# A transformer chain on one core: weight chunks held behind the latest gelu, late chunks packed into four periods, low weight parts from DRAM

## The chip, the core and the metric

The kernel runs on one core of one Trainium2 chip. The metric is the device time of one launch in microseconds; smaller is better. The program has five engines that run their own instruction queues in order: TensorE (PE, matmuls and transposes), VectorE (DVE), ScalarE (ACT), GpSimd (POOL) and SyncE (SP, which here issues nearly all DMA transfers). They wait for each other by semaphores.

## The reference

```python
attn = softmax(rotate(q) @ rotate(k).T / sqrt(64)) @ v          # 4 batches, 8 heads, 576 tokens
h = gelu(x @ w_in); u, v = h[..., :512], h[..., 512:]            # x: [4, 576, 512]
v_s = w_sg @ (layernorm(v) * g_ln) + b_sg
x = x + (u * v_s) @ w_out                                        # the gated block
u = x + (x.T @ U @ V).T
out = u + relu(u @ w_ch1) @ w_ch2                                # the channel block, 512 -> 2048 -> 512
```

All inputs are float32; weights reach the kernel as 64-bit words.

## The kernel before

**Stages.** Attention fills the first 320 us, the gated block (one batch after the other) runs to about 545 us, the channel block to the end. Every float32 operand is split into a high part (rounded) and a low part (the rest), and a product is three matmuls: high by high, low by high, high by low. High parts are copies on ACT, low parts subtractions on DVE or POOL.

**Weight chunks.** `w_ch1` and `w_ch2` come as 64-bit words, and DVE turns them into float32. One chunk is a DMA load of raw words, an `Abs` on ACT (`begin`, line 774 of before), and four DVE instructions (`rest`, lines 770 to 773). After two chunks (four of the late ones, which are half as large) `combine` makes four sums (lines 781 to 784), and the seven operands of one Strassen-like scheme go to DRAM (`COMBO`, tile `cb`, `cb3`). 26 chunks are converted during the gated block by `first_weights`; there a scheduler chooses each engine's order by its own time model, and `issue_after(x)` makes it put an instruction behind `x` on the same engine. The other 12 half chunks are converted during the channel block at the times of the table `LATE`.

**The gated block's v step.** `v_step` multiplies, ACT applies gelu out of PSUM (`ug<-v`, line 578, which frees the PSUM tile), DVE takes mean and variance (`bst`, `bmv`), POOL the reciprocal root (`brs`), ACT normalises (line 640) and copies the high part (`VH`). `u_step` has its gelu at line 659. `o_step` accumulates `w`, `y_step` transposes it (`t`, copies `YH` on ACT) and `z_step` multiplies the transposes.

**The channel block.** It has 12 periods of 14 steps, one product of 12 matmuls each; period i handles token block p and hidden group g of `ORDER[i]`. Steps 0 to 6 make `u @ w_ch1` (operands `UOP` times `W1`, into PSUM tiles rx, ry, rz), steps 7 to 13 the second product (`ROP` times `W2`, into aX, ry, rz). Between them DVE and ACT build `ROP` in a strict chain: at step time 1.0 ACT copies rx ("p1", PE's step 2 may write rx only then), at 2.0 DVE adds it to ry (tile `t`), at 2.5 ACT applies relu, at 3.0 ACT copies rx again ("u2", PE's step 4 waits), at 4.0 ACT copies rz ("p5", step 5 waits), at 5.0 DVE adds rx to it (step 6 waits). In this block all engines but PE follow an order written out by hand: each action has a time in steps, `at(t, fn)`, and the list sorted by time is each engine's program order; an engine reaches an action when its queue does, not at that time.

**Weights of the next period.** `split` loads operands from `COMBO` into a staging tile (`YH`, `YL`: four tiles in rotation), ACT copies the high part and the low part is made from the same staging tile. For a hidden group that was used before ("not fresh": the changes into the groups of periods 4, 5, 7 and 8), low parts listed in `KEPT` come from DRAM (`LOWS`) instead, written there in periods 0 to 2. Before the change these were two of the seven low parts of `W1` and all of `W2`; POOL made the other five of `W1` after r7l in the second half of periods 3, 4, 6 and 7. `UKEPT` keeps the token operands (`u` in the DMA rows) the same way at the times of `KEEP`.

Of the kernel before, what the change touches and what calls it, by code (L numbers as in the profile page):

```python
# [12 lines left out]
AF = mybir.ActivationFunctionType  # L13
# [52 lines left out]
def tile_kernel(ctx: ExitStack, tc: tile.TileContext, qk, vv, tabs, w_in, g_ln, wsgT, b_sg, w_out, u_r, v_r, w1, w2, out):  # L66
    nc = tc.nc

    def f(ap):
        return ap.bitcast(F32)  # L70

    def h2(ap):
        return ap.rearrange("p (a b) -> p a b", a=2)
# [26 lines left out]
    HALF = S // 2  # L100
# [315 lines left out]
    for h in range(2, NH):  # L416
        t = NC * h
# [123 lines left out]

    LASTS, LAST_G, LAST_D = [None] * 3, [None], [None]
    TAILS = []
# [32 lines left out]
    def gelu(t, ps):  # L576

        nc.scalar.activation(t, ps, AF.Gelu_apprx_tanh)
        return t
# [72 lines left out]
    def u_step(b, k0):  # L652
        ps = ps_tile(f"u{b}_{k0}")
        pr = []
        for k in range(KT):
            wh, wl = WUH[:, k, k0 * P:(k0 + 1) * P], WUL[:, k, k0 * P:(k0 + 1) * P]
            pr += [(wh, XH[:, k]), (wh, XL[:, k]), (wl, XH[:, k])]
        mm3(ps, pr, 2)
        nc.scalar.activation(h2(ug[:, k0]), ps[:, :, :HALF], AF.Gelu_apprx_tanh)

# [90 lines left out]
    ORDER = [(0, 0), (0, 1), (0, 2), (1, 2), (1, 0), (1, 1), (2, 1), (2, 0), (2, 2), (2, 3), (0, 3), (1, 3)]  # L751
    KEPT = [(0, 0), (0, 1)] + [(1, j) for j in range(7)]
    LOWS = [[dram.tile([P, 7, FG], F32, name=f"lows{c}_{g}", bufs=1) for g in range(NG - 1)] for c in range(2)]
# [81 lines left out]
    def first_u():  # L835
# [15 lines left out]
    LATE = (  # L851
        (36.0, 42.1, "t"), (50.0, 56.1, "t"), (55.7, 57.8, "s"), (48.0, 59.2, "w"), (64.0, 70.1, "t"), (78.0, 84.1, "t"), (74.0, 85.8, "w"),
        (92.0, 98.1, "t"), (90.0, 101.7, "w"), (106.0, 112.1, "t"), (111.7, 113.6, "s"), (104.5, 115.0, "w"),
    )
    FIRST = {9: (-11, 1.3, 1.8), 10: (-10.9, 1.7, 2.1), 11: (-10.8, 2.2, 2.6), 12: (-10.7, 2.7, 3.1), 13: (3.2, 5.2, 5.6)}
    KEEP = {
        0: ((1, 8.0), (2, 9.0)), 1: ((6, 8.0), (5, 9.0)), 2: ((7, 0.1), (3, 1.0), (4, 2.0)), 4: ((1, 8.0), (2, 9.0)),
        5: ((6, 0.1), (5, 0.6), (7, 1.1), (3, 1.6), (4, 2.1)),
    }

    def channel(before):
# [15 lines left out]
        def wslot(c, x, j, n=1):  # L877
            if c == 0 and j >= 5:
                return seta[2 * (j - 5) + x]
            return (W1, W2)[c][x][:, j:j + n].rearrange("p a b -> p (a b)")  # L880
# [16 lines left out]
        def at(t, fn):  # L897
            events.append((t, len(events), fn))
# [48 lines left out]
        def period(i):  # L947
# [71 lines left out]
            if g not in [x for _, x in ORDER[:i]] and g < NG - 1:  # L1019
                for c, j in KEPT:  # L1020
                    at(o + (0.05 if c == 0 else 8.0 if i in (0, 2) else 3.5), lambda c=c, j=j: nc.sync.dma_start(LOWS[c][g][:, j], f(wslot(c, 1, j))))
            if h != g:
                fresh = h not in [x for _, x in ORDER[:i]]
                loads = (2.3, 4.0, 4.5, 6.5, 6.6) if i == 0 else (0.2, 0.3, 1.3, 2.4, 5.0) if i > 3 else (1.4, 1.8, 3.2, 3.5, 5.0)
                highs = (3.85, 5.45, 6.5, 9.0, 9.4) if i == 0 else (3.85, 4.75, 6.0, 7.0, 9.4)
                for c, j0, j1, load, t, lo, e in (
                    (0, 0, 2, loads[0], highs[0], 4.35, dve), (0, 2, 4, loads[1], highs[1], 10.3, pool),
                    (0, 4, 6, loads[2], highs[2], 11.6, pool), (0, 6, 7, loads[3], highs[3], 12.9, pool),
                    (1, 0, 2, loads[4] + (i == 8), highs[4], 14.5, dve), (1, 2, 4, 11.65, 13.0, 15.08, dve),
                    (1, 4, 6, 13.0, 15.1, 16.5, dve), (1, 6, 7, 13.6, 16.2, 17.1, dve),  # L1030
                ):
                    if fresh or (c, j0) not in KEPT:
                        split(c, h, j0, j1, o + t, stage, o + load, o + lo, e)
                    else:
                        split(c, h, j0, j1, o + t, stage, o + load, o + 7 * c + j1 + 0.05)
# [12 lines left out]
            def combo(n, a, b):  # L1048
# [5 lines left out]
                      "l4": 17.35, "h1": 1.7, "h2": 2.1, "h6": 6.3, "h5": 6.7, "h3": 9.9, "h7": 15.9, "h4": 16.8} if i < 4 else  # L1054
                     {"T5": 1.0, "T6": 1.5, "T7": 1.95, "T4": 2.4, "l1": 2.9, "l2": 3.35, "l6": 3.8, "l5": 4.6, "l7": 14.1, "l3": 14.55,
                      "l4": 15.0, "h1": 1.7, "h2": 2.1, "h6": 3.1, "h5": 4.1, "h3": 6.3, "h7": 7.2, "h4": 9.9})
            parts = {5: (b12, b11), 6: (b22, lambda: U[5]), 7: (b12, b22), 4: (b21, lambda: U[6])}
# [33 lines left out]
        def leave_combo(m):  # L1091
            c, r, _, _ = parts[m]
            nc.sync.dma_start(COMBO[c][NG - 1][:, :, r], cbs[m // 4])
        for m, (load, t, _) in enumerate(LATE):
            at(load, lambda m=m: fetch(m))
            at(t - 0.1, lambda m=m: begin(m))
            at(t, lambda m=m: raws[m][1]())
            if m % 4 == 3:
                at(t + 0.75, lambda m=m: combine(parts[m][0], cbs[m // 4]))
                at(t + 1.5, lambda m=m: leave_combo(m))  # L1100
        for i in range(len(ORDER)):
# [182 lines left out]
```

## Time and profile before

| quantity | value |
| --- | --- |
| median of 3 runs | 936.46 us (935.14 to 937.0) |
| the profiled execution, its own time | 932.18 us |
| its span (first to last instruction) | 930.4 us |
| PE busy in the span | 892.5 us (96%) |
| DVE, ACT, POOL busy | 749.5, 463.6, 427.3 us |
| granted TensorE clock, mean | 0.991 |

Times in the rows below count from the start of the span. A row "[1.99 <-ACT ug L578]" says that the engine stood idle 1.99 us before it, and which instruction released it.

### The profile page before, as it was taken

To read this page: it belongs to the slowest core of one execution; us is meant where nothing else is said; L and a number is where in the kernel's file an instruction comes from. 1 tells how busy PE (TensorE), PEld (TensorE's weight loads), DVE (VectorE), ACT (ScalarE), POOL (GpSimd) and SP (SyncE) were. 2 spreads that over 40 slices of the span, in tenths; PEclk is the share of its full clock that TensorE was granted. 3 is DMA by queue.
4 is the path that set the end of the run, shared out by engine and by line. 5 is a ranking of instruction groups with operands and counts; after the bars stand their busy time and mean duration, and the time that the engine had idled before them with its cause. 6 is when DMAs were issued, how large, how long until landed. Compare 5 with 4: busy or idle time off the path is not lost. (4 is left out here: it accounts for less than half of the span.)

```text
span 930.4 us, 14303 instructions
## 1 busy us (share of the span) xinstructions
PE 892.5 (96%) x5279; PEld 804.7 (86%) x5279; DVE 749.5 (81%) x991; ACT 463.6 (50%) x719; POOL 427.3 (46%) x322
## 2 busy tenths in 40 slices
PE   8999999999999998899999988999999998999998
PEld 4677888888887998798999978999988998989997
DVE  6667788889997497897899988799778975897557
ACT  4556566666675643425334455553564355444232
POOL 6997777877645574232324434140414041441010
PEclk9999999999999998899999999999999999999999
DMA  6787776888751503544354257953669246737721
GB/s 188 203 204 185 200 198 165 219 190 156 184 155 40 172 16 98 173 132 131 129 172 147 80 193 243 306 197 119 217 237 371 71 158 242 237 90 268 277 96 68
DMA packets 96866, 161.18 MB, mean 173 GB/s; under 512 B 32326, under 2 KB 50012, under 8 KB 96796
## 3 DMA queue, kind: packets, MB, share of 16 engines
q1 hardware_dynamic: 96496, 160.19, 56.8%
q8 instruction: 42, 0.69, 0.3%
q14 instruction: 28, 0.23, 0.1%
q10 hardware_dynamic: 300, 0.08, 0.0%
HBM read 104.83 MB, written 37.56 MB: 153 GB/s over the span
## 5 line engine op out<-in xcount | busy, mean ns | idle before, releaser
L213 DVE TENSOR_REDUCE MX<-sm 128x1 f32<-128x576 f32 (+1 forms) x160 | 117.1, 748 | 37.9 <-PE sm L208 33.3
L277 PE MATMUL pv<-pc,VV 128*65 128x288 f32 (+1 forms) x516 | 145.7, 405 | 0.0
L250 PE MATMUL st<-Q,K 65*128 65x288 f32 (+3 forms) x640 | 126.4, 320 | 2.2 <-ACT pc L253 0.8
L250 PEld LDWEIGHTS st<-Q,K 65*128 65x128 f32 (+3 forms) x640 | 95.1, 178 | 16.7 <-DVE MX L213 1.4
L253 ACT ACTIVATE pc<-st 128x576 f32<-128x576 f32 x129 | 83.2, 646 | 30.2 <-PE st L250 27.8
L277 PEld LDWEIGHTS pv<-pc,VV 128*65 128x65 f32 (+1 forms) x516 | 69.3, 136 | 29.2 <-issue 0.2
L830 POOL TENSOR_TENSOR r1l<-t,r1h 128x768 fp32r<-128x768 f32 x12 | 22.7, 1891 | 135.2 <-ACT r1h L827 135.2
L830 POOL TENSOR_TENSOR r7l<-tmp,r7h 128x768 fp32r<-128x768 f32 x12 | 25.0, 2080 | 125.5 <-issue 60.2
L208 PE MATMUL sm<-K,Q 128*128 128x288 f32 (+1 forms) x320 | 72.0, 315 | 1.7 <-DMA Q<-Q 0.7
L172 POOL TENSOR_TENSOR Q<-raw,Q 128x576 fp32r<-128x576 f32 x30 | 45.1, 1504 | 27.8 <-ACT Q L167 27.7
L208 PEld LDWEIGHTS sm<-K,Q 128*128 128x128 f32 (+1 forms) x320 | 50.0, 178 | 8.0 <-ACT Q L167 1.0
L153 POOL TENSOR_TENSOR raw<-raw,tab 128x576 f32<-128x576 f32 x31 | 50.0, 1614 | 3.1 <-DMA raw<-in_qk 3.1
L774 ACT ACTIVATE cb<-raw 128x512 f32<-128x512 f32 x26 | 17.4, 673 | 64.1 <-DMA raw<-in_w 63.3
L330 DVE TENSOR_TENSOR X<-stage,rb 64x576 f32<-64x576 f32 x30 | 47.2, 1576 | 1.5 <-DMA rb<-rr 1.0
L155 POOL TENSOR_TENSOR raw<-raw 128x576 f32<-128x576 f32 x31 | 48.1, 1552 | 0.6
L587 PE MATMUL u<-XH,setA 128*128 128x288 f32 x256 | 46.2, 296 | 0.0
L154 POOL TENSOR_TENSOR raw<-raw,tab 128x576 f32<-128x576 f32 x31 | 44.6, 1437 | 0.0
L587 PE MATMUL v<-setA,XH 128*128 128x512 f32 x128 | 39.6, 390 | 0.0
L540 POOL TENSOR_TENSOR GL<-g,GH 128x576 fp32r<-128x576 f32 x16 | 25.8, 1613 | 30.0 <-ACT GH L673 30.0
L587 PEld LDWEIGHTS u<-XH,setA 128*128 128x128 f32 x256 | 38.4, 189 | 0.3
L431 POOL TENSOR_TENSOR XL<-X,XH 128x576 fp32r<-128x576 f32 x16 | 27.4, 1733 | 22.2 <-ACT XH L428 22.2
L293 ACT ACTIVATE stage<-pv 65x576 f32<-65x576 f32 x31 | 20.1, 647 | 29.6 <-PE pv L277 29.6
(1150 smaller groups left out, 2531.7 us busy)
## 6 DMA issues: line engine op xcount, KB each, us to landing
raw<-in_qk SPq DMA_DIRECT2D x31, 576.0 KB
combo<-cb SPq DMA_DIRECT2D x16, 896.0 KB
raw<-in_w SPq DMA_DIRECT2D x26, 512.0 KB
YH<-combo SPq DMA_DIRECT2D x21, 512.0 KB
YL<-combo SPq DMA_DIRECT2D x21, 512.0 KB
K<-Q SPq DMA_DIRECT2D x30, 288.0 KB
u<-setA SPq DMA_DIRECT2D x16, 384.0 KB
w2l<-lows SPq DMA_DIRECT2D x12, 512.0 KB
```

What stands on the lines that cost most here:

```text
L153: lambda: e.tensor_tensor(raw[:, 0], raw[:, 0], tab[:, 0], ALU.mult),
L154: lambda: e.tensor_tensor(raw[:, 1], raw[:, 1], tab[:, 1], ALU.mult),
L155: lambda: e.tensor_tensor(raw[:, 0], raw[:, 0], raw[:, 1], ALU.add),
L172: nc.gpsimd.tensor_tensor(Q2[:, :S], rot, f(Q1), ALU.subtract)
L208: nc.tensor.matmul(ps[:TS[t], n, :HALF], Q1[:, t * P:t * P + TS[t]], K1[:, n * HALF:(n + 1) * HALF], start=True, stop=True)
L213: nc.vector.tensor_reduce(MXs[h % 2][:TS[t], t:t + 1], ps[:TS[t], :, :HALF], AX.XY, ALU.max)
L250: nc.tensor.matmul(ps[:kk, n, :HALF], l[:, c * P:c * P + kk], r[:, ns], start=st, stop=not st)
L253: nc.scalar.activation(h2(pc[:kk]), ps[:kk, :, :HALF], AF.Exp, scale=0.125)
L277: nc.tensor.matmul(o, l, r, start=(c == 0 and j == 0), stop=(c == NC - 1 and j == len(pr) - 1))
L330: nc.vector.tensor_tensor(X[b][rows, pr], STAGE.pop(h - 1 + a)[:D], RB[i][:, a], ALU.mult)
L587: nc.tensor.matmul(o, l, rr, start=(first and j == 0), stop=(last and j == n - 1))
L830: return e.tensor_tensor(out, a, b, ALU.subtract)
```

## The change

`LAST_D` gets a second entry, which every gelu (of `v_step` and `u_step`) sets; `first_weights` already put its chunk behind whatever `LAST_D` holds, so the chunk's `Abs` now also stands behind the latest gelu on ACT. `LATE` is rewritten: the 12 half chunks stand in the first three steps of periods 4 (four chunks), 6, 7 (two each) and 8 (four), with all `Abs` of one period at its start. `KEPT` holds all seven low parts of `W1`: five more DRAM writes of 256 KB in each of periods 0 to 2, five more loads in each of periods 3, 4, 6 and 7, and 20 POOL subtractions fewer. Two token operands are kept in period 2 instead of 1. The last two high copies of `W2` move from 15.1 and 16.2 to 13.2 and 14.2 where the weights are not fresh, the first of `W1` from 3.85 to 4.1.

```diff
-    LASTS, LAST_G, LAST_D = [None] * 3, [None], [None]
+    LASTS, LAST_G, LAST_D = [None] * 3, [None], [None, None]
...
-        nc.scalar.activation(t, ps, AF.Gelu_apprx_tanh)
+        LAST_D[1] = nc.scalar.activation(t, ps, AF.Gelu_apprx_tanh)
...
-    KEPT = [(0, 0), (0, 1)] + [(1, j) for j in range(7)]
+    KEPT = [(c, j) for c in range(2) for j in range(7)]
...
-        (36.0, 42.1, "t"), (50.0, 56.1, "t"), (55.7, 57.8, "s"), (48.0, 59.2, "w"), (64.0, 70.1, "t"), (78.0, 84.1, "t"), (74.0, 85.8, "w"),
-        (92.0, 98.1, "t"), (90.0, 101.7, "w"), (106.0, 112.1, "t"), (111.7, 113.6, "s"), (104.5, 115.0, "w"),
+        (50.0, 56.05, "t"), (40.0, 56.8, "w"), (55.7, 57.5, "s"), (55.8, 58.2, "s"), (78.0, 84.05, "t"), (70.0, 84.8, "w"),
+        (92.0, 98.05, "t"), (88.0, 98.8, "w"), (106.0, 112.05, "t"), (102.0, 112.8, "w"), (111.7, 114.1, "s"), (111.8, 114.8, "s"),
...
-        0: ((1, 8.0), (2, 9.0)), 1: ((6, 8.0), (5, 9.0)), 2: ((7, 0.1), (3, 1.0), (4, 2.0)), 4: ((1, 8.0), (2, 9.0)),
+        0: ((1, 8.0), (2, 9.0)), 2: ((6, 3.0), (5, 3.5), (3, 4.0), (7, 9.0), (4, 10.0)), 4: ((1, 8.0), (2, 9.0)),
...
+                tops = (15.1, 16.2) if fresh else (13.2, 14.2)
...
-                    (1, 4, 6, 13.0, 15.1, 16.5, dve), (1, 6, 7, 13.6, 16.2, 17.1, dve),
+                    (1, 4, 6, 13.0, tops[0], 16.5, dve), (1, 6, 7, 13.6, tops[1], 17.1, dve),
...
-            at(t - 0.1, lambda m=m: begin(m))
+            at(math.floor(t) + m % 4 / 100, lambda m=m: begin(m))
...
-                at(t + 1.5, lambda m=m: leave_combo(m))
+                at(t + 1.7, lambda m=m: leave_combo(m))
```

PE's order is unchanged. ACT's order in the gated block, at the second batch's v step, before the change (`ug<-v` and `ug<-u` are gelus, `cb<-raw` a chunk's `Abs`):

```order
L578 ACTIVATE ug<-v_0_3787 128x1024
L774 ACTIVATE cb<-raw 128x2x256
L640 ACTIVATE ug<-ug,bmv,brs 128x512 x2
L578 ACTIVATE ug<-v_2_3838 128x1024
L642 ACTIVATE VH<-ug 128x512
L774 ACTIVATE cb<-raw 128x2x256
L642 ACTIVATE VH<-ug 128x512
L640 ACTIVATE ug<-ug,bmv,brs 128x512 x2
L642 ACTIVATE VH<-ug 128x512 x2
L774 ACTIVATE cb<-raw 128x2x256
L659 ACTIVATE ug<-u_0_4017 128x576
```

The same place after the change:

```order
L579 ACTIVATE ug<-v_0_3787 128x1024
L775 ACTIVATE cb<-raw 128x2x256
L641 ACTIVATE ug<-ug,bmv,brs 128x512 x2
L643 ACTIVATE VH<-ug 128x512
L579 ACTIVATE ug<-v_2_3838 128x1024
L775 ACTIVATE cb<-raw 128x2x256
L643 ACTIVATE VH<-ug 128x512
L775 ACTIVATE cb<-raw 128x2x256
L641 ACTIVATE ug<-ug,bmv,brs 128x512 x2
L643 ACTIVATE VH<-ug 128x512 x2
L660 ACTIVATE ug<-u_0_4017 128x576
```

The first `Abs` shown was the third chunk's, ahead of gelu `v_2`; now it is the second chunk's, and the third chunk's stands behind that gelu. The gelu `u_0` has come out from behind the fifth chunk's `Abs`.

ACT's order where period 7 begins (`tmp<-r7x` are the copies p1 and u2, `cb` a late chunk's `Abs`, `w2h` high copies of `W2`), before:

```order
L827 ACTIVATE w2h<-YH 128x1024
L774 ACTIVATE cb_7164<-t_7575 128x256
L827 ACTIVATE tmp<-r7x 128x768
L827 ACTIVATE w2h<-YL 128x1024
L827 ACTIVATE w2h<-YH 128x512
L827 ACTIVATE t_7730<-t_7730 128x768
L827 ACTIVATE tmp<-r7x 128x768
L827 ACTIVATE r1h<-t_7730 128x768
L774 ACTIVATE cb_7752<-words 128x256
L827 ACTIVATE w1h<-YL 128x1024
```

After:

```order
L828 ACTIVATE w2h<-YL 128x1024
L828 ACTIVATE w2h<-YH 128x1024
L775 ACTIVATE cb_7426<-t_7585 128x256
L775 ACTIVATE cb_7426<-words 128x256
L828 ACTIVATE w2h<-YL 128x512
L828 ACTIVATE tmp<-r7x 128x768
L828 ACTIVATE t_7740<-t_7740 128x768
L828 ACTIVATE tmp<-r7x 128x768
L828 ACTIVATE r1h<-t_7740 128x768
L828 ACTIVATE tmp<-r7z 128x768
```

The new tile `cb_7752`, which the old order opened behind r1h, is gone from this place; both chunks and two more high copies stand ahead of p1, and p5 (`tmp<-r7z`) follows r1h directly.

SP's order in period 4 before, from the first kept low part on (`u` are kept token operands, `t` a raw chunk):

```order
L931 DMA w1l<-lows_1_3325 128x1024
L918 DMA YH<-combo_1_3345 128x512
L1093 DMA combo_3_3347<-cb_6618 896x1x256
L918 DMA YL<-combo_1_3349 128x1024
L1082 DMA t_7050<-in_w 128x512
L1018 DMA u_1_3337<-setA_72 128x768 x2
L1018 DMA u_2_3338<-setA_73 128x768 x2
L931 DMA w2l<-lows_1_3328 128x1024 x2
L918 DMA YH<-combo_1_3349 128x1024
```

After:

```order
L932 DMA w1l<-lows_1_3325 128x1024
L919 DMA YL<-combo_1_3345 128x512
L1095 DMA combo_3_3347<-cb_6897 896x1x256
L932 DMA w1l<-lows_1_3325 128x1024
L919 DMA YH<-combo_1_3349 128x1024
L932 DMA w1l<-lows_1_3325 128x512
L932 DMA setA_71<-lows_1_3325 128x512
L932 DMA setA_73<-lows_1_3325 128x512
L1019 DMA u_1_3337<-setA_72 128x768 x2
L1019 DMA u_2_3338<-setA_73 128x768 x2
L932 DMA w2l<-lows_1_3328 128x1024 x2
L919 DMA YL<-combo_1_3349 128x1024
```

The chunk's load `t` ahead of the kept operands is gone, and four low loads stand in between.

## Rows read from the trace of the kernel before

**Rows 1.** Windows by channel period 2 to 8 (from first matmul): length, PE, PEld, DVE, ACT, POOL busy, clock.

```profile
613.89:643.41 29.52, 29.52 (x169) 29.25 (x169) 27.28 (x28) 14.53 (x20) 4.54 (x3) 1.00 0.60 214
643.41:674.24 30.83, 30.14 (x169) 29.50 (x169) 25.58 (x31) 14.69 (x19) 11.06 (x7) 1.00 0.51 164
674.24:706.29 32.05, 30.52 (x169) 29.25 (x169) 25.81 (x36) 16.63 (x23) 11.09 (x7) 1.00 0.78 268
706.29:738.42 32.13, 30.24 (x169) 29.17 (x169) 27.06 (x32) 16.71 (x23) 4.03 (x2) 1.00 0.58 218
738.42:769.14 30.72, 30.09 (x169) 29.45 (x169) 23.46 (x31) 13.91 (x19) 11.04 (x7) 1.00 0.47 149
769.14:804.49 35.35, 31.80 (x170) 30.90 (x170) 25.17 (x32) 17.39 (x24) 11.41 (x7) 0.95 0.66 222
804.49:836.99 32.50, 30.45 (x169) 29.20 (x169) 27.28 (x38) 16.30 (x23) 11.00 (x7) 1.00 0.45 147
```

**Rows 2.** Chain of waits in period 7: start, duration, what.

```profile
773.68 7.23 DMA combo<-cb
...
783.06 3.61 PE r7z L906 x12
```

**Rows 3.** Timeline of PE: start, duration, line, instruction, idle before and its releaser.

```profile
359.75 0.53 PE L587 MATMUL w<-GH,WOH 128*128 128x288 f32 x2 [1.99 <-ACT ug L578]
...
375.55 0.80 PE L727 MATMUL z<-YH,U 128*128 128x512 f32 x1 [2.72 <-ACT YH L711]
...
819.78 2.38 PE L906 MATMUL r8x<-XL,setA 128*128 128x384 f32 x12 [1.64 <-DVE tmp L969]
```

**Rows 4.** Timeline of ACT where periods 7 and 8 begin.

```profile
768.65 1.06 ACT L827 ACTIVATE w2h<-YH 128x1024 fp32r<-128x1024 f32 x1 [5.08 <-PE a6X L906]
769.61 0.42 ACT L774 ACTIVATE cb<-t 128x256 f32<-128x256 f32 x1
771.52 0.82 ACT L827 ACTIVATE tmp<-r7x 128x768 f32<-128x768 f32 x1 [1.49 <-PE r7x L906]
...
803.24 1.06 ACT L827 ACTIVATE w2h<-YH 128x1024 fp32r<-128x1024 f32 x1 [3.98 <-DMA YH<-combo]
```

**Rows 5.** Windows of DVE, tile cb alone, in period 7: one late chunk, then one combine.

```profile
770.10:771.76 1.66, 1.43 (x4) 1.00 0.91 279
771.76:773.60 1.84, 1.61 (x4) 1.00 0.94 289
```

**Rows 6.** Timeline of DVE in period 8.

```profile
814.26 2.09 DVE L781 TENSOR_TENSOR cb<-cb 128x256 f32<-128x256 f32 x1
```

**Rows 7.** Timeline of POOL in period 8.

```profile
814.22 1.85 POOL L830 TENSOR_TENSOR r1l<-t,r1h 128x768 fp32r<-128x768 f32 x1 [11.74 <-ACT r1h L827]
```

**Rows 8.** Timeline of ACT in the gated block, 355 to 375 us.

```profile
356.23 0.69 ACT L774 ACTIVATE cb<-raw 128x512 f32<-128x512 f32 x1 [6.75 <-DMA raw<-in_w]
...
358.70 1.00 ACT L578 ACTIVATE ug<-v 128x1024 f32<-128x1024 f32 x1
...
373.38 0.67 ACT L774 ACTIVATE cb<-raw 128x512 f32<-128x512 f32 x1 [6.59 <-DMA raw<-in_w]
```

**Rows 9.** Timeline of DVE in the gated block, 352 to 358 us.

```profile
352.09 0.42 DVE L770 TENSOR_SCALAR cb<-cb 128x512 f32<-128x512 f32 x1
...
353.61 1.28 DVE L633 BATCH_NORM_STATS2 bst<-ug 128x6 f32<-128x512 f32 x2
...
357.02 0.23 DVE L639 SCALAR_TENSOR_TENSOR bmv<-bmv,brs 128x1 f32<-128x1 f32 x2 [0.27 <-POOL brs L636]
```

**Rows 10.** Timeline of SP's queue at the end of period 7.

```profile
798.00 0.32 SPq L918 DMA_DIRECT2D YH<-combo  x1
...
801.39 0.32 SPq L931 DMA_DIRECT2D w2l<-lows  x1
```

**Rows 11.** Windows, columns as in rows 1, last two DMA share and GB/s.

```profile
556.00:560.00 4.00, 1.78 (x10) 1.41 (x10) 1.71 (x3) 2.83 (x5) 1.27 (x1) 1.00 0.02 7
...
800.00:805.00 5.00, 4.72 (x27) 4.44 (x27) 5.00 (x6) 1.38 (x2) 2.47 (x2) 1.00 0.94 322
```

More of the change, by code (lines that the diff above doesn't have):

```diff
@@ L1 @@
+import math
 from contextlib import ExitStack
@@ L658, in u_step @@
         mm3(ps, pr, 2)
-        nc.scalar.activation(h2(ug[:, k0]), ps[:, :, :HALF], AF.Gelu_apprx_tanh)
+        LAST_D[1] = nc.scalar.activation(h2(ug[:, k0]), ps[:, :, :HALF], AF.Gelu_apprx_tanh)
     def s_step(b, d):
@@ L1020, in period @@
                 for c, j in KEPT:
-                    at(o + (0.05 if c == 0 else 8.0 if i in (0, 2) else 3.5), lambda c=c, j=j: nc.sync.dma_start(LOWS[c][g][:, j], f(wslot(c, 1, j))))
+                    at(o + (0.05 if c == 0 else 8.0 if i == 0 else 6.0 if i == 2 else 3.5), lambda c=c, j=j: nc.sync.dma_start(LOWS[c][g][:, j], f(wslot(c, 1, j))))
             if h != g:
@@ L1024, in period @@
                 loads = (2.3, 4.0, 4.5, 6.5, 6.6) if i == 0 else (0.2, 0.3, 1.3, 2.4, 5.0) if i > 3 else (1.4, 1.8, 3.2, 3.5, 5.0)
-                highs = (3.85, 5.45, 6.5, 9.0, 9.4) if i == 0 else (3.85, 4.75, 6.0, 7.0, 9.4)
+                highs = (3.85, 5.45, 6.5, 9.0, 9.4) if i == 0 else (3.85, 4.75, 6.0, 7.0, 9.4) if i == 1 else (4.1, 4.75, 6.0, 7.0, 9.4)
+                tops = (15.1, 16.2) if fresh else (13.2, 14.2)
                 for c, j0, j1, load, t, lo, e in (
@@ L1054, in period @@
                       "l4": 17.35, "h1": 1.7, "h2": 2.1, "h6": 6.3, "h5": 6.7, "h3": 9.9, "h7": 15.9, "h4": 16.8} if i < 4 else
-                     {"T5": 1.0, "T6": 1.5, "T7": 1.95, "T4": 2.4, "l1": 2.9, "l2": 3.35, "l6": 3.8, "l5": 4.6, "l7": 14.1, "l3": 14.55,
-                      "l4": 15.0, "h1": 1.7, "h2": 2.1, "h6": 3.1, "h5": 4.1, "h3": 6.3, "h7": 7.2, "h4": 9.9})
+                     {"T5": 1.0, "T6": 1.5, "T7": 1.95, "T4": 2.4, "l1": 2.9, "l2": 3.35, "l6": 3.8, "l5": 4.6, "l7": 14.02, "l3": 17.4,
+                      "l4": 16.9, "h1": 1.7, "h2": 2.1, "h6": 3.1, "h5": 4.1, "h3": 6.3, "h7": 7.2, "h4": 9.9})
             parts = {5: (b12, b11), 6: (b22, lambda: U[5]), 7: (b12, b22), 4: (b21, lambda: U[6])}
```

## The prediction

> **What bounds the kernel now.** I read the channel block by periods first: windows cut at each period's first matmul [rows 1]. Periods 1, 2 and 9 to 11 are matmuls without a gap; period 2 has 29.52 us with PE busy for all of them, 2.11 us a step. The reader is to see how much longer periods 3 to 8 are: 1.31, 2.53, 2.61, 1.20, 5.83 and 2.98 us, 16.5 together. That is all this part of the change can give back. Then the chain of waits, for what the longest gap hangs on [rows 2], and the timelines of PE, ACT, DVE and SP around each gap.
>
> Two things make the gaps. The first is a collision in period 7. A finished weight set is written to DRAM in 7.23 us [rows 2]; the next half chunk wants the same staging tile (`cb3`, one buffer), so ACT's `Abs` waits for the write, and p5 stands behind it on ACT. PE waits before step 5, and then runs slowly: 3.61 us for a product of 2.11. The granted clock over the period is 0.95 [rows 1], so between its two levels, 2.4 and 1.2 GHz, it fell for a short while after that wait. The second is DVE at a period's start: late chunks stand ahead of the addition to ry, so relu is late, so u2 behind it on ACT is late, and PE's step 4 waits; or a chunk and its combine stand ahead of the addition at 5.0, and step 6 waits, as for 1.64 us in period 8 [rows 3].
>
> In the gated block two gaps have one cause [rows 3, 8]: an `Abs` that waits 6.75 us for its raw words stands ahead of gelu v_2, and PE waits 1.99 us for the PSUM tile; another that waits 6.59 us stands ahead of gelu u_0 and of the copies YH, and PE waits 2.72 us.
>
> **The change part by part.** Durations: a late chunk costs DVE 1.43 us and a combine 1.61 [rows 5]; an `Abs` 0.42, a high copy of two operands 1.06, p1 and its like 0.82 on ACT, of which some 0.1 overlaps the next [rows 4].
>
> *Period 3* loses its chunk. DVE's additions then start 1.43 us sooner, more than the 1.31 that the period is too long. Gain 1.3.
>
> *Period 5* loses its chunk, and the load of a raw chunk that held SP back in period 4 ahead of the kept operands; four weight loads and the first high copy of `W2` then come in time. The addition to ry then runs when ry is ready. Step 6 still has DVE at its edge (one low part waits for ACT), so I take 2.4 of 2.61.
>
> *Period 6* has both chunks ahead of the addition as before, but two subtractions (l3, l4) now stand behind it. Gain 1.2.
>
> *Period 7* loses the collision: its set is written and the next chunk is 12 steps away. But both chunks and the combine now stand ahead of the addition: DVE is free of the last period's sums 1.2 us in, chunks and combine take 2 x 1.43 + 1.61, the first waits some 0.6 us for its `Abs`, so the addition ends 7.4 us in, relu 0.8 later, u2 0.8 after that at 9.0, where step 4 begins at 8.5. That leaves 0.6, with a slower first product (2.38 for 2.11 [rows 3]) 0.9. Gain 4.9.
>
> *Period 4* has three chunks ahead of the addition (before: two, with waits for `Abs`). The first starts at 2.6 behind two high copies and an `Abs`; three chunks and the addition end at 7.9, u2 at 9.5: step 4 is 1.1 late, with the slower product 1.3. The fourth chunk and the combine end before step 6 needs DVE. Gain 2.5 - 1.3 = 1.2.
>
> *Period 8* has two chunks before and two with the combine after the addition. The chunks end 9 us in; the combine then meets POOL's r1l. In the trace one of its operations took 2.09 us instead of 0.40 while r1l ran for 1.85 [rows 5 to 7]. So the addition at 5.0 ends about 14.2 us in, where step 6 begins at 12.7: the old wait of 1.64 stays at 1.6. Gain 0.9, from the earlier part of the period.
>
> Whether that combine meets r1l again decides 1.7 us. The first operation of a combine took 2.09 us once and about 0.4 in the other two late combines; by their mean the collision would cost 0.6 and period 8 would gain 2.0, the whole sum 12.9. I take the collision as certain, since both follow r1h and the last chunk by less than 1 us. The Trainium skill, "SBUF — State Buffer", section "Who interferes with whom", says the same by mechanism: a DVE instruction with two SBUF inputs is blocked for the whole of a GpSimd instruction that reads SBUF. By that rule the sum is the lower one.
>
> *The 20 POOL subtractions* that go lay in the second halves of periods 3, 4, 6 and 7, where PE works through; DVE's own work there and PE's hide them. I count nothing for them but the staging tiles, which ACT's copies now free early. *The 15 added writes and 20 added loads*, 256 KB each at 322 GB/s [rows 11], are 0.8 us of DMA apiece, 4.1 a period. In periods 1 to 4, 6 and 7 DMA is 0.47 to 0.78 busy [rows 1], and 4.1 of 30 us fit; the loads are issued in steps 4 to 7 and needed ten steps later. In period 0 five writes come ahead of a load whose copy ACT reaches at about 560 us. DMA stood idle just before, 0.02 busy from 556 to 560 [rows 11], so most of the 4.1 falls into that hole: a loss of 0.6, bounds 0 and 4.1.
>
> *The top copies* of `W2` move ahead of p1. In period 8's start: the first copy's 512 KB were issued at 798.0 and landed at 803.2 [rows 4, 10]. Behind them go 512 + 512 + 256 KB, 4.1 us at 322 GB/s, so the last lands at 807.3, 2.8 us into the period; its copy takes half of 1.06, p1 0.8, which ends at 4.2, exactly where step 2 begins. I put 0.2 us on each of four periods, 0.8. Bounds: 0, and 3.4 each if the added loads lie in front (below).
>
> *The gated block.* DVE's new order puts the statistics of v_0 ahead of the second chunk, at 352.1 instead of 353.6; with the chunk operations now in between, `bmv` is ready at about 355.5 instead of 357.0 [rows 9], normalising and one copy on ACT take 2.2, so gelu v_2 starts at 357.9, not 358.7 [rows 8]: 0.8 gained at 359.75. All behind it shifts with DVE, the raw words of the fifth chunk too; gelu u_0 no longer stands between its `Abs` and the copies YH, 0.55 more. The `Abs` itself still does, so most of the 2.72 stays. Gain 1.3; bounds 0 and 4.7, both waits.
>
> **The sum** against the profiled span: 1.3 + 1.2 + 2.4 + 1.2 + 4.9 + 0.9 in periods 3 to 8 is 11.9; plus 1.3, less 0.6 and 0.8: 11.8 us. Span 930.4 to 918.6, the profiled execution's 932.18 to 920.4. The median of the runs lies 4.28 above that execution; I take the same difference off it: 936.46 - 11.8 = 924.7.
>
> **The rivals.** *Packed periods wait as before.* Only the collision goes (5.83 down to the 2.5 to 3 of periods 4 and 8, 3.1 us), with periods 3 and 5, 3.7; 4, 6 and 8 keep what they have and the gated block gives nothing: 6.8 less 1.4, so 931.1. For it: DVE has as many chunk operations as before, in fewer places. Against: periods 3 and 5 lose theirs altogether.
>
> *Slower: the last top copy is late.* Place: ACT at the start of periods 4, 5, 7 and 8, where p1 now stands behind the copy. If 4.1 us of added low loads still lie in the queue in front of it, p1 ends 4.1 late, step 2 waits 4 us, four times 16 less the 11.8: 940.7. It decides from 3 us of lateness a period. Against: those loads are issued three steps before the copies' own. The Trainium skill, "DMA: Bandwidth & Descriptors", section "Latency and other measured facts", gives HBM access latency as 0.2 us on average and 2 us at high load; no run here shows it, and 2 us more on that load, an estimate from that page, would give about 931.
>
> *Even.* Period 0 loses its 4.1 and half of the lateness comes, 8: 936.2.
>
> *Larger.* The gated waits go in full (3.4 more), period 8 meets no r1l (1.7) and period 4 none of its wait (1.3): 918.3. For it: a shorter wait at 359.75 may keep the clock up behind it.
>
> **How the numbers follow.** Forecast (gain 8 to 15 us) 0.60; packed periods wait 0.20; larger 0.08; even 0.06; late top copies 0.06. Range 918.5 to 932.5, which leaves out the even and the late cases and part of the larger. A measurement tells 0.2%, 1.9 us: faster means under 934.6. Faster 0.88, same 0.06, slower 0.06.
>
> **What would show it.** Period 7 without any wait of ACT on `combo<-cb`, at 30.4 us; periods 3, 5 and 6 within 0.3 of 29.5; period 8 still with a wait of 1 to 2 us before its step 6 behind a stretched combine; p1 never ending later than 4.4 us into periods 4, 5, 7, 8; POOL with two instructions in those halves; gelu v_2 0.8 us sooner. Wrong if step 2 shows waits on `tmp` behind `w2h`, if period 0 is over 40 us, or if new waits stand in the gated block, where a scheduler's order moved at many places.

## The result and the profile after

The changed kernel takes 925.64 us (median of 4 runs, 924.77 to 927.18) beside 935.8 (934.29 to 937.0) for the kernel before on the same chip: a ratio of 0.9894, interval 0.9873 to 0.9915, 10.2 us faster. The forecast was 924.7. Its profiled execution took 925.63 us with a span of 923.6; the span before was 930.4, so the two traces differ by 6.8 us, not by 10.2. What follows is read from the traces.

Windows of the changed kernel, periods 1 to 8, cut at each period's first matmul (columns as in [rows 1]):

```profile
586.27:619.27 33.00, 31.07 (x170) 30.76 (x169) 23.57 (x25) 15.77 (x20) 10.71 (x7) 0.95 0.66 224
619.27:648.80 29.53, 29.53 (x170) 29.25 (x169) 27.28 (x28) 13.77 (x18) 4.35 (x2) 1.00 0.82 309
648.80:678.30 29.50, 29.50 (x170) 29.50 (x169) 24.23 (x27) 16.48 (x21) 3.98 (x2) 1.00 0.63 213
678.30:707.90 29.60, 29.60 (x171) 29.35 (x170) 26.70 (x40) 15.47 (x23) 4.04 (x2) 1.00 0.95 335
707.90:739.90 32.00, 29.92 (x170) 29.13 (x169) 25.77 (x28) 16.94 (x23) 3.97 (x2) 1.00 0.56 214
739.90:769.40 29.50, 29.50 (x170) 29.50 (x169) 23.45 (x31) 14.86 (x19) 3.96 (x2) 1.00 0.65 204
769.40:799.20 29.80, 29.73 (x169) 29.41 (x168) 22.46 (x32) 16.43 (x23) 3.98 (x2) 1.00 0.83 294
799.20:830.40 31.20, 30.17 (x170) 29.55 (x170) 28.24 (x41) 16.50 (x24) 10.99 (x7) 1.00 0.52 169
```

Beside [rows 1], periods 3, 4, 6 and 7 are now clean or nearly so. Period 5 is as long as before, period 8 is 1.3 shorter, and period 1, which had no gap before (29.4 us), is 33.0. The granted clock of 0.95 over that period means that it fell to the lower of its two levels for a while, as in period 7 before. The timeline of PE names the waits (the first four here are in the gated block):

```profile
359.30 0.53 PE L588 MATMUL w<-GH,WOH 128*128 128x288 f32 x2 [1.39 <-ACT ug L579]
...
373.96 0.80 PE L728 MATMUL z<-YH,U 128*128 128x512 f32 x1 [3.19 <-ACT YH L712]
...
435.17 0.49 PE L728 MATMUL z<-YH,U 128*128 128x512 f32 x1 [2.17 <-ACT YH L712]
437.86 0.79 PE L728 MATMUL z<-YL,U 128*128 128x512 f32 x1 [2.19 <-DVE YL L718]
...
598.87 1.95 PE L907 MATMUL r1z<-XH,setA 128*128 128x384 f32 x8 [1.93 <-ACT tmp L828]
...
714.21 0.61 PE L907 MATMUL r5x<-setA,w1h 128*128 128x384 f32 x2 [1.95 <-ACT tmp L828]
...
812.94 2.38 PE L907 MATMUL r8x<-XL,setA 128*128 128x384 f32 x12 [0.90 <-DVE tmp L970]
```

The first two answer to [rows 3]: the wait at 359 is 0.6 shorter and the z step of the second batch begins 1.6 us earlier. Then the third batch loses 4.4 us in two waits, where the kernel before lost 1.0 and, 8 us later, another 1.8, which is gone now. What stands behind three of these waits is on ACT:

```profile
430.78 0.68 ACT L775 ACTIVATE cb<-raw 128x512 f32<-128x512 f32 x1 [7.16 <-DMA raw<-in_w]
431.37 1.49 ACT L579 ACTIVATE ug<-v 128x1024 f32<-128x1024 f32 x2
433.54 0.67 ACT L775 ACTIVATE cb<-raw 128x512 f32<-128x512 f32 x1 [0.68 <-DMA raw<-in_w]
434.10 1.93 ACT L712 ACTIVATE YH<-t 128x1024 fp32r<-128x1024 f32 x2
...
597.06 1.06 ACT L828 ACTIVATE w1h<-YH 128x1024 fp32r<-128x1024 f32 x1 [2.67 <-DMA YH<-combo]
598.02 0.79 ACT L828 ACTIVATE tmp<-r1z 128x768 f32<-128x768 f32 x1
...
712.83 0.63 ACT L828 ACTIVATE w2h<-YL 128x512 fp32r<-128x512 f32 x1 [1.99 <-DMA YL<-combo]
713.37 0.79 ACT L828 ACTIVATE tmp<-r5x 128x768 f32<-128x768 f32 x1
```

The pattern is the same three times: ACT stands before an instruction whose load has not landed, and the copy that frees PE's PSUM tile is queued behind it. At 430.78 it is a chunk's `Abs`, ahead of two gelus and of the copies YH; at 597.06 the first copy of the next `W1`, ahead of p5; at 712.83 the last top copy of `W2`, ahead of p1. In the kernel before, the chunk's `Abs` stood ahead of the first of these gelus too, but its words had come 1.6 us earlier:

```profile
429.20 0.67 ACT L774 ACTIVATE cb<-raw 128x512 f32<-128x512 f32 x1 [7.87 <-DMA raw<-in_w]
```

SP's queue says when these loads were issued:

```profile
586.54 3.65 SPq L1022 DMA_DIRECT2D lows<-w1l  x5
590.24 1.46 SPq L1022 DMA_DIRECT2D lows<-setA  x2
591.80 0.46 SPq L919 DMA_DIRECT2D YH<-combo  x1
...
705.69 0.61 SPq L919 DMA_DIRECT2D YL<-combo  x1
```

The load of period 1 comes behind seven writes of kept low parts, five of them added by the change. SP takes 5.1 us to issue the seven, so the load is issued 5.5 us into the period, and its copy starts at 597.06; the one of period 5 takes from 705.69 to 712.8 while DMA is 0.95 busy over period 4. In period 8 the row of [rows 6] is still there, at the same meeting with POOL:

```profile
807.64 1.99 DVE L782 TENSOR_TENSOR cb<-cb 128x256 f32<-128x256 f32 x1
```

```profile
807.50 1.85 POOL L831 TENSOR_TENSOR r1l<-t,r1h 128x768 fp32r<-128x768 f32 x1 [15.96 <-ACT r1h L828]
```

### The profile page after: what moved, and what is told of

It reads as the page before. It is cut to its first block, busy times and chain, and to the rows that moved or that the text cites. A ratio compares the mean times of both kernels' runs of the same rounds, so it can differ in the third digit from the quotient of the medians.

```text
span 923.6 us, 14340 instructions
## 1 busy us (share of the span) xinstructions
PE 888.6 (96%) x5279; PEld 805.5 (87%) x5279; DVE 747.8 (81%) x991; ACT 465.9 (50%) x719; POOL 397.6 (43%) x302
## 4 chain that ended last, share of the span: by engine, by line
PE 41%; DVE 11%; DMA 3%; issue 2%; ACT 2%; POOL 1%; SPq 0%; DVEq 0%; ACTq 0%; POOLq 0%
PE w L588 2%; PE u L588 2%; PE m L588 2%; DMA YL<-combo 1%; DVE cb L773 1%; DVE cb L774 1%; PE a8X L907 1%; PE a5X L907 1%; PE a2X L907 1%; PE a11X L907 1%; PE a3X L907 1%; PE a10X L907 1%; PE a9X L907 1%; PE a7X L907 1%; PE r11x L907 1%
## 5 line engine op out<-in xcount | busy, mean ns | idle before, releaser
L254 ACT ACTIVATE pc<-st 128x576 f32<-128x576 f32 x129 | 83.3, 646 | 31.2 <-PE st L251 29.0
L173 POOL TENSOR_TENSOR Q<-raw,Q 128x576 fp32r<-128x576 f32 x30 | 46.2, 1540 | 29.8 <-ACT Q L168 29.7
L294 ACT ACTIVATE stage<-pv 65x576 f32<-65x576 f32 x31 | 20.1, 647 | 29.7 <-PE pv L278 29.6
```

What stands on the lines that cost most here:

```text
L173: nc.gpsimd.tensor_tensor(Q2[:, :S], rot, f(Q1), ALU.subtract)
L254: nc.scalar.activation(h2(pc[:kk]), ps[:kk, :, :HALF], AF.Exp, scale=0.125)
```

## The experiments

All lengths of periods below are from first matmul to first matmul. Times of one kernel spread over 3 to 8 us between runs here (the kernel before: 930.42 to 941.52 in 17), so a difference of 2 us shows in the profile's periods rather than in a median.

**The copy behind p5.** Only the copy that p5 waited for in period 1 moves: the change had left it at 3.85 there (the program has no period 12).

```diff
-    highs = ... (3.85, 4.75, 6.0, 7.0, 9.4) if i == 1 else (4.1, 4.75, 6.0, 7.0, 9.4)
+    highs = ... (3.85, 4.75, 6.0, 7.0, 9.4) if i == 12 else (4.1, 4.75, 6.0, 7.0, 9.4)
```

> Only period 1 changes: the first high copy of the next W1 stands behind p5 on ACT (4.1 instead of 3.85), as in the other periods. Theory A (the 3.6 us that period 1 gained in length come from p5 standing behind a copy whose load lands late): p5 runs as soon as rz is ready, the wait of 1.93 us before step 5 goes, a wait of up to 0.8 us before step 6 can stay, since the low part that DVE makes of the same load stands ahead of the addition at 5.0; period 1 from 33.0 to 29.5 to 30.5, the time from 925.6 to 922.3 to 923.4. Theory B (the late load stops DVE just as long, wherever the copy stands): the wait moves to step 6, period 1 stays over 32, the time within 1 us of 925.6.

926.74 us, ratio 0.9918 [0.9892, 0.9944]; period 1 took 31.4 us. It lies between the theories. ACT and DVE show why:

```profile
593.29 0.81 ACT L828 ACTIVATE tmp<-r1z 128x768 f32<-128x768 f32 x1 [0.49 <-PE r1z L907]
595.35 1.06 ACT L828 ACTIVATE w1h<-YH 128x1024 fp32r<-128x1024 f32 x1 [1.24 <-DMA YH<-combo]
```

```profile
596.44 1.23 DVE L831 TENSOR_TENSOR w1l<-YH,w1h 128x1024 fp32r<-128x1024 f32 x1 [4.55 <-ACT w1h L828]
597.58 0.95 DVE L970 TENSOR_TENSOR tmp<-r1x,tmp 128x768 f32<-128x768 f32 x1
```

p5 now runs when rz is ready. But the low part of the same load stands ahead of the addition at 5.0 on DVE, and step 6 waits 1.13 us. With the order on ACT mended some of the loss is left, and what is left hangs on the same late load. How much the order alone costs, the length doesn't tell: with the early copy the period took 33.8, 31.1 and 34.0 us in three other executions, each with a wait of 1.3 to 2.6 us before step 5.

**The writes behind the loads.** The five added writes of period 1 are issued at step 6.2.

```diff
-    at(o + (0.05 if c == 0 else ...
+    at(o + (6.2 if c == 0 and j > 1 and i == 1 else 0.05 if c == 0 else ...
```

> Only period 1 changes: five of the seven writes of low parts of W1 (the five that the change added there) are issued at step 6.2, behind the five weight loads, instead of at the period's start. Theory A (these writes in the queue ahead of the first load are what makes it late): the load lands some 4 us sooner, ACT never waits for it, period 1 from 33.0 to about 29.5, the time about 922.3. Theory B (the load is late because of the reads of the last period, which the DMA engines still carry, or period 1 is long for another reason): the load still lands later than p5's time, period 1 stays over 32, the time within 1 us of 925.6.

925.8 us, ratio 0.9907 [0.9879, 0.9936]. Period 1 took 29.7 us and its wait is gone: the load is issued 2 instead of 7 writes behind the period's start, and the copy waits for nothing.

```profile
588.55 0.90 SPq L1022 DMA_DIRECT2D lows<-w1l  x2
590.65 0.32 SPq L919 DMA_DIRECT2D YH<-combo  x1
```

```profile
596.36 1.05 ACT L828 ACTIVATE w1h<-YH 128x1024 fp32r<-128x1024 f32 x1
```

Theory A holds for period 1. SP issues the load 2.3 us into the period instead of 5.5. The median did not show the gain. In the profiled execution other periods were longer: 31.0 in period 4, with a wait of 0.84 us before step 2 behind the last top copy, and 30.5 in period 2.

**The last top copy behind p1**, for the change from period 4 into period 5 alone.

```diff
-    tops = (15.1, 16.2) if fresh else (13.2, 14.2)
+    tops = (15.1, 16.2) if fresh else (13.2, 16.2) if i == 4 else (13.2, 14.2)
```

> Only the change from period 4 into period 5 is touched: the last of the three high copies of W2 goes back behind p1 (16.2). Theory A (period 5 stayed 2.5 us too long because p1 waits behind that copy, whose load lands 4.8 us into the period): the wait of 1.95 us before step 2 goes, period 5 from 32.0 to about 29.6, the time from 925.6 to 923.2. Theory B (period 5 is long, as before the change, for a reason on DVE, and the wait only shows at step 2 first): a wait of 1 to 2 us appears at step 4 or 6 instead, period 5 stays over 31, the time within 1 us of 925.6.

927.21 us, ratio 0.9925 [0.9898, 0.9951]. Period 5 took 30.3 us, against 32.0, 33.9, 32.0, 33.9 and 33.8 in five executions with the early copy (the three long ones have a granted clock of 0.95 over the period). p1 runs ahead of the copy, and the copy no longer waits:

```profile
713.60 0.79 ACT L828 ACTIVATE tmp<-r5x 128x768 f32<-128x768 f32 x1
...
715.76 0.62 ACT L828 ACTIVATE w2h<-YL 128x512 fp32r<-128x512 f32 x1
```

The wait before step 2 is gone, one of 0.29 before step 6 is left. Theory A. Period 1, not mended here, took 33.8.

**No hold behind the latest gelu.** `LAST_D[1]` is not set in `gelu` and `u_step`.

> The changed kernel without the hold behind the latest gelu: chunks in the gated block are held by DVE's last instruction alone, as before. By the prediction's term the hold is worth 1.3 us: without it 926.9. By the trace of after, where a chunk's Abs that waited 7.16 us for raw words stands ahead of two gelus and of the copies YH in the third batch, the hold loses about 1.4 us in all: without it 924.2, with the wait of 2.2 us near 435 us gone and the waits near 360 and 375 us as in the kernel before. A third possibility is that the execution of before that was profiled ran its gated block faster than most: then the two are within 0.5 us.

926.4 us, ratio 0.9905 [0.9874, 0.9935]. The waits of the third batch, now at 438 and 446 us, are back to 0.76 and 1.93 us, those near 361 and 377 are 2.97 and 3.71. From the block's first matmul to the channel block's first matmul with a low weight part (545.45 in the kernel before) the gated block took 250.9 us, against 250.8 in the changed kernel: one pair decides nothing. All profiled executions together do. With the hold: 250.8, 251.3, 251.1, 251.5, 252.3, 251.6, 252.7, mean 251.6. Without it (the kernel before twice, this run, and three of the runs below): 249.5, 249.7, 250.9, 249.9, 250.5, 251.0, mean 250.2. The hold costs about 1.3 us; against the three of these that have the rest of the change (250.9, 250.5, 251.0) it is 0.8. By the time from the block's first matmul to the first z matmul of the second batch (mean 78.3 us with it, 80.1 without) it gives 1.8 us there, and takes 3.1 behind it.

**Low parts of W1 by POOL again**: `KEPT` as before, the rest as changed.

> The changed kernel with KEPT as before: five of the seven low parts of W1 are made by POOL from the staging tiles again, and the 15 added writes and 20 added loads go. Theory A (what the writes and loads cost is all in periods 1 and 5, by transfers that come late, and POOL's subtractions were hidden): period 1 back to 29.4, period 5 to about 30 without a wait before step 2, the others as after; about 920. Theory B (POOL holds the staging tiles up to 13 steps into the period, so the loads of the next copies are issued late, and the top copies, which now stand ahead of p1, with them): period 1 back to 29.4, but waits before steps 2 to 6 in periods 4, 5, 7 and 8, 1 to 3 us each; 925 to 930.

928.36 us, ratio 0.9924 [0.9897, 0.9951]. Period 1 is 29.3 and period 0 40.6 (40.8 in the changed kernel). Periods 4, 5, 7 and 8 are 31.3, 31.8, 31.7 and 32.8, together 5.0 more than in the changed kernel. Period 8 shows how:

```profile
807.53 0.63 ACT L828 ACTIVATE w2h<-YL 128x512 fp32r<-128x512 f32 x1 [1.81 <-DMA YL<-combo]
808.06 0.79 ACT L828 ACTIVATE tmp<-r8x 128x768 f32<-128x768 f32 x1
```

```profile
808.91 0.62 PE L907 MATMUL r8x<-setA,w1h 128*128 128x384 f32 x2 [1.66 <-ACT tmp L828]
```

In SP's queue the load of that copy was issued 2.0 us after the low load ahead of it (802.24 after 800.21) and 0.7 us before the period; in the changed kernel it was 0.4 us (796.98 after 796.57) and 2.2 us before. What it can stand for there is a free staging tile, which POOL's subtractions hold longer; that this is what SP waited for is read from the order, not shown. Theory B: the losses are where it put them, though period 5 is no longer than in the changed kernel. With POOL's low parts the early top copies lose.

**The new table alone**: the kernel before with `LATE`, the places of the `Abs` and the leaving write as changed. It has neither the hold, nor the added low parts, nor the moved copies.

> The kernel before with the new LATE table alone (with the places of the Abs and the leaving write that go with it). By the prediction's terms this part has nearly all of the gain: period 7 from 35.4 to 30.4, period 3 to 29.5, period 5 to about 29.7 to 32, periods 4, 6 and 8 as after or up to 1 us longer, period 1 at 29.4; the ratio to before 0.989 to 0.992. The rival is that the collision's 5 us only go when the low parts come from DRAM too (staging tiles free early): period 7 then stays over 32 and the ratio is 0.994 or more.

923.45 us, ratio 0.9875 [0.9844, 0.9906]: as fast as the whole change or faster. Periods 4 to 8, columns as above:

```profile
673.40:704.30 30.90, 30.13 (x170) 29.48 (x169) 27.07 (x40) 17.58 (x25) 11.06 (x7) 1.00 0.85 298
704.30:734.70 30.40, 29.95 (x170) 29.33 (x169) 26.13 (x28) 16.05 (x23) 4.36 (x2) 1.00 0.57 212
734.70:765.40 30.70, 30.06 (x170) 29.43 (x169) 23.45 (x31) 13.42 (x18) 11.06 (x7) 1.00 0.47 147
765.40:795.40 30.00, 29.97 (x171) 29.49 (x170) 22.55 (x32) 16.02 (x22) 11.06 (x7) 1.00 0.74 255
795.40:826.40 31.00, 29.90 (x169) 29.28 (x169) 28.10 (x41) 18.14 (x25) 11.19 (x7) 1.00 0.56 170
```

Period 7's collision goes by the table alone, period 5 gains 1.7 with the top copies at their old places, and period 6 stays at 30.7, as before. So the 1.2 us of period 6 come not from the chunks but from the two subtractions (l3, l4) that the whole change moves behind the addition (from 14.55 and 15.0 to 17.4 and 16.9, in lines that the diff above leaves out). The run with POOL's low parts, which moves them too, has 29.6 there. Here they still stand ahead of it on DVE, u2 is late, and PE waits 0.62 us before step 4:

```profile
737.96 0.95 DVE L831 TENSOR_TENSOR XL<-X,XH 128x768 fp32r<-128x768 f32 x1
...
740.28 0.95 DVE L831 TENSOR_TENSOR XL<-YL,XL 128x768 fp32r<-128x768 f32 x1
741.14 0.95 DVE L970 TENSOR_TENSOR t<-r6y,tmp 128x768 f32<-128x768 f32 x1
```

Period 4 is 1.3 longer than in the changed kernel, with a wait of 0.77 us before step 4. DVE's first chunk starts 2.4 us into the period, behind its `Abs`; in the changed kernel (second row) 1.1 us:

```profile
675.69 0.29 DVE L771 TENSOR_SCALAR cb<-cb 128x256 f32<-128x256 f32 x1 [1.25 <-ACT cb L775]
```

```profile
679.42 0.28 DVE L771 TENSOR_SCALAR cb<-cb 128x256 f32<-128x256 f32 x1
```

Periods 0 to 10 together (544.0 to 896.2 before, 543.3 to 885.4 here) gain 10.1.

**The last combine behind the addition at 5.0**, its write with it.

```diff
-    at(t + 0.75, ... combine(...))
-    at(t + 1.7, ... leave_combo(m))
+    at(t + (2.25 if m == 11 else 0.75), ... combine(...))
+    at(t + (3.1 if m == 11 else 1.7), ... leave_combo(m))
```

> Only period 8 changes: the last combine and its write come after the addition at 5.0 on DVE (5.05 instead of 3.55), out of the way of POOL's r1l. If the combine in front of that addition, stretched by r1l, is what step 6 of period 8 waits for, its wait of 0.9 goes and the period is 29.6 to 30.2 instead of 31.1; the time falls by 1 to 1.5. If period 8 is long for its two chunks and the waits at its start, it stays at 31 or gains 0.3. A loss of up to 4 us is possible where the first load of the next weights, which now waits for the later write, comes late to its copy.

925.8 us, ratio 0.9903 [0.9874, 0.9933]. The combine's first operation took 0.41 us, not 1.99, and step 6 did not wait. But period 8 took 31.0 us:

```profile
813.48 1.23 DVE L831 TENSOR_TENSOR w1l<-YH,w1h 128x1024 fp32r<-128x1024 f32 x1 [2.36 <-ACT w1h L828]
...
815.49 0.41 DVE L782 TENSOR_TENSOR cb<-cb 128x256 f32<-128x256 f32 x1
```

```profile
807.22 0.61 PE L907 MATMUL r8x<-setA,w1h 128*128 128x384 f32 x2 [0.39 <-ACT tmp L828]
...
822.96 0.59 PE L907 MATMUL a8X<-r6h,w2h 128*128 128x384 f32 x2 [0.71 <-DVE X L991]
```

The collision is real, and moving the combine gained next to nothing. DVE now stands 2.36 us ahead of the addition, waiting for the first copy of the next `W1`, which ACT makes behind p5; the addition ends 13.1 us into the period instead of 13.7. The combine's 1.7 us then stand ahead of the operands of the next steps, and PE waits for DVE's sum three steps further on, at 822.96. The wait of 0.39 us before step 2 is behind a late top copy again. So this run shows what the move gives, 0.2 us, and not what a combine without the collision in its old place would give.

**Two mends together**: the writes as in the second run, the last top copy at 16.2 everywhere.

> Two mends together: the five added writes of period 1 behind the weight loads, and the last high copy of W2 behind p1 again in all four changes to weights used before. If the two losses are independent, period 1 is 29.5 to 29.7 and period 5 30.0 to 30.5 in the same execution, with periods 4, 7 and 8 never over 30.0, 30.2 and 31.3; the sum of the twelve periods is 4.5 to 6 us below the changed kernel's and the ratio to before 0.983 to 0.986. If the time lost there only moves on to the next period, the sum falls by less than 2.

922.47 us, ratio 0.9866 [0.9834, 0.9898]. Period 1 is 30.0 and period 5 30.3, periods 4 and 7 are 29.4 and 29.6, and period 8 is 31.0. Periods 0 to 10 took 339.6 us instead of 344.1, 4.5 less: the two losses are independent. Period 2 took 30.6, which takes 1.1 back. The row is the old pattern at another place: a copy of `W2` waits for its load, ahead of relu and u2 on ACT.

```profile
623.22 1.06 ACT L828 ACTIVATE w2h<-YH 128x1024 fp32r<-128x1024 f32 x1 [1.26 <-DMA YH<-combo]
```

**Three alterations**: the two mends, the same five writes of period 0 at step 6.7, and no hold.

> The changed kernel with three things altered: the last high copy of W2 behind p1 in all changes to weights used before, five of the seven added writes behind the weight loads in period 1 and in period 0, and no hold behind the latest gelu. From the executions profiled so far: twelve periods 339.6 with the first two, the gated block (from its first matmul to the channel block's) 250.1 without the hold instead of 251.6: together 1.5 below the run with the two mends alone, 921, ratio to before 0.983 to 0.987. If the hold were worth the prediction's 1.3, the gated block would be 251 to 253 and the time 924.

920.33 us, ratio 0.9831 [0.9794, 0.9868], faster than both kernels. The gated block took 250.5 us, period 1 29.7 and period 5 29.9.

**A chunk held behind YH.** The same kernel, with `LAST_D[1]` set by the copy YH in `y_step`.

> The run before with a chunk of the gated block held behind the latest copy YH on ACT instead of the latest gelu. In the order of ACT the Abs that stood ahead of gelu u_0 and both copies YH in the second batch comes out from there. If the wait of 2.2 to 3.7 us before the first z matmul of the second batch (near 376 us) hangs on this Abs, it goes and the gated block falls from 250.1 to 247 to 248; the time is about 919. If PE then waits for DVE's sums or for u instead, because the chunk's raw words hold DVE as long, the gated block stays at 249.5 to 251.

917.4 us, ratio 0.9795 [0.9751, 0.9839], the lowest median of all; its interval overlaps that of the run before. The gated block took 248.6 us. The wait near 376 did not go; it changed its engine. First the run with three alterations, then this one:

```profile
376.23 0.79 PE L728 MATMUL z<-YH,U 128*128 128x512 f32 x1 [3.57 <-ACT YH L712]
```

```profile
376.77 0.80 PE L728 MATMUL z<-YL,U 128*128 128x512 f32 x1 [2.72 <-DVE YL L718]
```

The copies YH are early now, but DVE has a chunk and a combine in front of YL. By 437 us 0.3 of the 1.9 is gained; the rest lies between 437 and 531, 94.1 us instead of 95.6, and is not explained wait by wait here.

**Both late top copies at their old places**, with the three alterations.

> The run with the three alterations, and both late high copies of W2 at their old places, 15.1 and 16.2, everywhere. If the early first copy (13.2) is worth something, the periods with chunks at their start are longer: 4 near 30.9 and 8 over 32, as DVE then waits for the copy with its low part; 1 to 3 us slower than the run with the three alterations. If it is worth nothing, the twelve periods are 339 to 340 again.

920.97 us, ratio 0.9838 [0.9799, 0.9877]. Periods 0 to 10 took 338.3 us, against 338.8 in the run with three alterations; period 4 29.8, period 8 31.2. With low parts from DRAM the early first copy is worth nothing that these runs can tell.

**The kernel before, again.**

> The kernel before, unchanged, for the spread between executions: the attention part ends between 294 and 298 us in all executions profiled so far. Gated block 249.5 to 251, period 1 at 29.4, periods 3 to 8 together 191 to 195, period 7 with its wait on the write of the chunk set. If the gated block comes out over 251.5, the hold's loss is not shown.

935.39 us, ratio 0.9997 [0.9968, 1.0027]. Gated block 249.7, period 1 30.1, periods 3 to 8 together 193.6 (193.6 in the first profile), the wait before step 5 of period 7 3.23 us.

## Why the prediction was right, and where not

The time came out 0.9 us from the forecast. The main mechanism was right: the collision and most of the waits at the periods' starts go with the new table, and the table alone gave the whole gain (923.45 us). The other three parts of the change together added nothing that the medians tell. By the forecast's own terms, span against span:

| term | forecast | traces |
| --- | --- | --- |
| period 3 | +1.3 | +1.3 |
| period 4 | +1.2 | +2.5 |
| period 5 | +2.4 | +0.1 |
| period 6 | +1.2 | +1.2 |
| period 7 | +4.9 | +5.6 |
| period 8 | +0.9 | +1.3 |
| p1 late in four periods | -0.8 | in the rows above |
| period 0 | -0.6 | -0.4 |
| period 1 | 0 | -3.6 |
| gated block | +1.3 | -1.3 |
| sum | 11.8 | 6.7 |

**Right.** The collision in period 7 was the largest piece, and it went by the table alone (the run with the table). Period 3 lost its chunk and its gap. Period 6 gained what was forecast for it, and by the step named: the two subtractions behind the addition. Period 8 kept a wait before step 6 behind a combine that met r1l, 0.90 us instead of the 1.6 forecast.

**Period 8, the collision.** The prediction took it as certain, and it came: 1.99 us for an operation that takes 0.42, and 0.41 once the combine stood elsewhere. The Trainium skill, "SBUF — State Buffer", section "Who interferes with whom", has a DVE instruction with two SBUF inputs contend with a GpSimd instruction that reads SBUF; these rows agree. What it would give to avoid it is not shown: the rival put 1.7 us on it, and the run with the combine moved gained 0.2, but there the combine stood in the way of later steps.

**Period 4, mis-sized.** The forecast left 1.3 us of lateness before step 4, from "The first starts at 2.6 behind two high copies and an `Abs`". In the changed kernel the first chunk started at 1.1, since the first of these copies lay 2.0 us ahead of the period, and u2 ended at 8.3, before step 4. In all ten executions with low parts of `W1` from DRAM there was no wait before step 4 of period 4; in the two with the same table and POOL's low parts there was one (0.77 and 0.49 us, chunks from 2.4 and 3.0). So the extra 1.3 us come with the low parts from DRAM, for which the prediction counted nothing "but the staging tiles, which ACT's copies now free early". That this is the step in between fits the rows and is not shown by itself.

**Period 5, where a rival came true.** The table alone took 1.7 us off this period, with the top copies at their old places. In the whole change the early last copy took nearly all of it back. What failed is the term of 0.2 us per period for the top copies: the last one landed 4.9 us into period 5, not 2.8, and p1 ended 6.3 us in, not 4.2. That is p1 behind a late copy, as in the rival that ended slower, in one period of four; the prediction's own sign of being wrong, step 2 waiting on `tmp` behind `w2h`, was there. In other executions with the early copy the same wait came in periods 4, 7 and 8 too (up to 0.84, 0.85 and 0.52 us); in the four with the copy at 16.2 it came in none. The rival's reason, the added low loads in front, is not shown: the run without them waits 1.76 us at the same place, with a load issued later (0.3 us ahead of the period instead of 2.2). The prediction's bound of 3.4 us allowed for this; the load was estimated at the rate of the loads ahead of it, without the stand of SP's queue (it issued nothing from 702.4 to 705.3, ahead of a low load of `W2` that precedes this one) and without the kept operands and words issued behind it. From 700 to 714 us the DMA engines were busy all the time.

**Period 1, missing.** The prediction placed the added writes in periods 0 to 2 and looked at period 0 alone; the sentence "4.1 of 30 us fit" judged the others by DMA's mean share. But the writes stand at the period's first step, in front of a load that has three steps to land, and SP alone needs 3.2 us more until it issues that load (5.5 us into the period instead of 2.3). The mean over a period said nothing about these three steps. Period 0, for which a loss of up to 4.1 was allowed, lost nothing that can be told: 40.2 to 41.0 us in seven executions with the writes first, 40.4 to 40.7 in four without them. So the sign "if period 0 is over 40 us" said nothing, as it held before the change.

**The gated block, wrong sign.** "Gelu v_2 0.8 us sooner" came in part: in the second batch it started at 358.24 instead of 358.70, 0.6 us sooner counted from the block's first matmul. The step that failed is "All behind it shifts with DVE, the raw words of the fifth chunk too": in the third batch the chunks' raw words came later than before (the `Abs` at 430.78, before at 429.20), and their `Abs` stood ahead of gelus and YH there. New waits in the gated block were the third sign of being wrong that the prediction named. The term rested on two waits of one batch out of four.

**What stays open.** The medians moved by 10.2 us, the traces by 6.8. Both profiled executions of the kernel before (932.18 and 932.08 us) lie in the lower part of its spread, whose median is 935.5; the profiled executions of the other kernels lie on both sides of theirs. The longer executions tend to have the lower clock: seven of 25 executions of the kernel before have a mean granted clock of 0.985 to 0.988 and take 937.9 us on average, the others, at 0.989 or more, 935.1. At which place a long execution loses its time was not seen. The forecast used the difference of 4.28 as an offset; with it, terms that were 5 us too large in sum met a median that moved 3.4 more than the traces. That the number came so close is luck. Period 2 was 30.5 to 30.6 in three runs with the writes moved, 29.6 in two others with them, and 30.9 once without the added writes. In all four long ones ACT waited 1.2 to 1.6 us for a load of `W2`; why that load landed later there is open.

## What to carry to other kernels

A transfer that "fits" by its share of a period is not free: ask what stands behind it in the queue, and how many steps that load has. An in-order engine that waits for a load holds every PSUM copy queued behind it, so a copy that may be late belongs behind those that release the matmuls; then see what the other engine does with the same load. When work is moved out of the way of one wait on an engine that is busy nine tenths of the time, look for the wait again a few steps later.

## What was not expected of the hardware

The attention part is the same program in all kernels here, yet the gated block's first matmul came between 294.4 and 297.7 us in 14 profiled executions. A wait of PE on a DMA transfer near 74 us of 0.5 to 2.7 us stands in eight of them, whose mean is 296.7; in the other six it is 0.4 us or less, and the mean is 295.3. And a 512 KB load with seven writes in front of it took 5.3 us from its issue to the copy that waited for it (591.80 to 597.06), a 256 KB load 7.1 us (705.69 to 712.83); by size at 322 GB/s [rows 11] they are 1.6 and 0.8 us.
